# Finer parts of a weight split, earlier scatters and later transposes in a three-stage kernel

## The chip, the cores and the metric

The kernel runs on one core of one Trainium2 chip. The metric is the device time of one execution in microseconds; the time of a kernel is the median of several runs.

## The reference, cut to what matters

Three stages are chained over 4608 tokens of width 512. Attention without a softmax gives the rows `x`. A layer of eight experts adds to each row whose skip score is positive the gated output of its best expert. A dense layer follows, with the silu of one product between two. The inputs of the dense layer, `w_in` and `w_out`, are float64; the device reads them as pairs of 32-bit words.

```python
def _moe_ref(x, w_skip, w_gate, w1, w2):
    do_compute = (x @ w_skip) > 0
    xc = x[do_compute]
    ...
    for e in range(8):
        h = np.maximum(xc[mask] @ w1[e], 0.0)
        y[mask] = gate_w[mask, None] * (h @ w2[e])
    out[do_compute] = xc + y
def _moe2_ref(x, w_in, w_out):
    h = x @ w_in
    g = h * (1.0 / (1.0 + np.exp(-h)))
    return g @ w_out
```

## The kernel before, in words

The attention stage (to about 155 us) also sorts the tokens by expert. It stays as it is. What follows is one loop over **steps** (`steps`, the loop over `n` at the end). Steps 0 to 63 belong to eight **units** of eight steps, one unit per expert (`units`, kind "e"; unit 0 is steps 0 to 7). A unit has 384 down to 256 rows in three tiles (two in the last unit). From step 64 on come nine **groups** of 512 tokens and sixteen steps each (kind "g", the dense or GLU layer).

A step uses one **chunk** of weights: 128 of the hidden columns. In step n the tensor engine (PE) runs the first product of step n (`first`, L1194, twelve matmuls into `ph`), then the second product of step n - 1 (`second`, L1224, three matmuls per tile into `acc`). Each product is made of three, because both operands are split into a rounded part and a rest (`w[:, 0]`, `w[:, 1]`; `x` and `h` likewise). `h` leaves `ph` by ACT (L1200, the relu) and the vector engine DVE (L1201, the rest); in a GLU step by ACT, DVE, ACT, DVE in turn (L1206 to L1209). At the end of a unit DVE adds the result to the rows (`xe`, L1234); the rows are stored by a DMA on POOL's queue (L1239, units 0 to 5) or on SP's queue, and gathers on POOL's queue (L906, `fetch`) bring the rows of the unit after next into the buffers so freed.

**The weights.** SP's queue loads them into three staging buffers in the order of the list `order`, three tasks ahead (`load_ahead`). An expert's chunk is split by ACT (L143) and DVE (L144), two steps before its use. A chunk of the dense layer comes in two float64 **halves** (`w_in`, `w_out`). A half takes ACT's L153 and DVE's L154, L156, L158, L162, L166, then ACT's L177, two products on POOL (L178, L179) and one addition on DVE (L174). The `yield`s of `split` cut DVE's operations into parts. `split_on` issues L177 to L179 for halves whose parts are all issued, and L174 at its next call. Eleven chunks of the dense layer (22 halves) have buffers of their own and are split during the expert steps. The table `at_step` says when: whole halves in one go, at the third, fifth and seventh step of units 0 to 6, and one more at step 55. The other ten halves follow from step 64, by `split_slowly`, four parts of five a step.

**Turns.** The rows of the next unit are transposed on PE into `pt` (`turn`, L1149; two `pt` buffers), copied by ACT (L1158) and DVE (L1159) into `xT`. A unit's four turns come at its sixth step (one), seventh (two) and eighth (one), ahead of that step's first product; all four of unit 7 at its last step.

**Scatters.** `permute(t)` writes the place of 128 rows into the table `perm` by an indirect DMA on POOL's queue (L1138); six of them, at steps 2, 4, ... 12. Each writes the same tensor, so each waits until the one before has landed. The table is read back at step 24.

The schedule is manual: every engine executes its instructions in the order in which the program issues them. In a step that order is: turns, first product with its evictions, `split_on`, second product (in a unit's first step: the stores and gathers of the unit before), weight splits, then the scatter.

```python
        split_on()
        if n >= LAG:
            u2, f2, c2 = steps[n - LAG]
            second(u2, f2, c2, hs.pop(n - LAG))
            ...
        split_next(len(at_step.get(n, [])))
        if n >= NE:
            split_slowly(LAST_OPS)
```

Of the kernel before, what the change touches and what calls it, by code (L numbers as in the profile page):

```python
# [24 lines left out]
def tile_kernel(ctx, tc, q, k, v, g_norm, w_skip, w_gate, w1, w2, w_in, w_out, out):  # L25
# [3 lines left out]
    E = w_gate.shape[1]  # L29
# [13 lines left out]
    KD = DM // P  # L43
# [9 lines left out]
    KE = FE // P  # L53
# [3 lines left out]
    NWA = 3  # L57
# [27 lines left out]
    NP = GT + -(-CAPS[E - 1] // P)  # L85
# [51 lines left out]
    def split(task):  # L137


        t = staged.pop(task)  # L140
        w = part(task)
        if task[1] is None:
            nc.scalar.activation(w[:, 0, :], t.bitcast(F32), AF.Copy)  # L143
            nc.vector.tensor_tensor(w[:, 1, :], t.bitcast(F32), w[:, 0, :].bitcast(F32), ALU.subtract)  # L144
            yield
            return
        tv = t.rearrange("p (n o) -> p n o", o=2)
        hi, lo = tv[:, :, 1], tv[:, :, 0]
        vec = nc.vector
        x1 = xp.tile([P, DM], F32, tag="x", name="x1")  # L150
        x3 = xp.tile([P, DM], F32, tag="x", name="x3")
        x2 = xp.tile([P, DM], F32, tag="x", name="x2")
        nc.scalar.activation(x3, lo.bitcast(U32), AF.Copy, scale=2.0 ** -52)  # L153
        vec.tensor_scalar(x2.bitcast(I32), hi, 0x7FFFFFFF, None, ALU.bitwise_and)  # L154
        yield
        vec.scalar_tensor_tensor(x1, x2, SMALLEST, hi.bitcast(F32), ALU.is_ge, ALU.mult)  # L156
        yield
        vec.tensor_scalar(  # L158
            x2.bitcast(I32), x1.bitcast(I32), 3, 0x3FFFFFFF, ALU.logical_shift_left, ALU.bitwise_and
        )  # L160
        yield
        vec.scalar_tensor_tensor(  # L162
            x1.bitcast(I32), x1.bitcast(I32), -0x40000000, x2.bitcast(I32), ALU.bitwise_and, ALU.bitwise_or
        )
        yield
        vec.tensor_scalar(x2.bitcast(I32), x1.bitcast(I32), -0x800000, None, ALU.bitwise_and)  # L166
        begun.append((w, x1, x2, x3))
        yield
# [12 lines left out]

    NE = E * KE
    NCW = 2 * (NW - NWE)
    at_step = {}
    for n in range(NE - NWA):
        at_step.setdefault(n + 1, []).append((n + NWA, None))
    for i in range(NCW):
        n = (i // 3) * KE + 2 + 2 * (i % 3) if i < NCW - 1 else NE - KE - 1  # L190
        at_step.setdefault(n, []).append((NE + i // 2, i % 2))

    LAST_OPS = 4
    order = [(c, None) for c in range(NWA)] + [x for n in sorted(at_step) for x in at_step[n]]
    order += [(NE + i // 2, i % 2) for i in range(NCW, 2 * KF)]
    nload = [0]
    nsplit = [0]
# [15 lines left out]
    def split_slowly(n):  # L213
        while n:
            if not slow:
                if nsplit[0] == len(order):
                    return
                slow.append(split(order[nsplit[0]]))
                nsplit[0] += 1
            if next(slow[0], slow) is slow:  # L220
                slow.clear()
                split_on()
                load_ahead()
            else:
                n -= 1

# [922 lines left out]
    def turn(u, kk, pt=None):  # L1151
        if pt is None:
            pt = ps_t.tile([P, GN], F32, tag="t", name="pt")
            for s in range(len(tokens_of[u])):
                turn_tile(u, kk, s, pt)
        x = xtp.tile([P, 2, GN], F32R, tag="xT", name="xT")
        n = sum(tokens_of[u])
        nc.scalar.activation(x[:, 0, 0:n], pt[:, 0:n], AF.Copy)  # L1158
        nc.vector.tensor_tensor(x[:, 1, 0:n], pt[:, 0:n], x[:, 0, 0:n].bitcast(F32), ALU.subtract)  # L1159
        xT_of[u, kk] = x  # L1160
# [25 lines left out]
    def first(u, f, c):  # L1186
        kind, _ = units[u]
        n = sum(tokens_of[u])
        w = chunks[c]
        ph = ps_h.tile([P, GN], F32, tag="h", name="ph")  # L1190
        for kk in range(KD):
            x = xT_of[u, kk]
            for a, (wi, xi) in enumerate(((0, 0), (0, 1), (1, 0))):
                nc.tensor.matmul(  # L1194
                    ph[:, 0:n], w[:, wi, kk * P:(kk + 1) * P], x[:, xi, 0:n],
                    start=(kk == 0 and a == 0), stop=(kk == KD - 1 and a == 2),
                )
        h = hp_.tile([P, 2, GN], F32R, tag="h", name="h")
        if kind == "e":
            nc.scalar.activation(h[:, 0, 0:n], ph[:, 0:n], AF.Relu)  # L1200
            nc.vector.scalar_tensor_tensor(  # L1201
                h[:, 1, 0:n], ph[:, 0:n], 0.0, h[:, 0, 0:n].bitcast(F32), ALU.max, ALU.subtract
            )
        else:
            sg = sgp.tile([P, GN], F32, tag="sg", name="sg")
            nc.scalar.activation(sg, ph, AF.Sigmoid)  # L1206
            nc.vector.tensor_tensor(sg, ph, sg, ALU.mult)  # L1207
            nc.scalar.activation(h[:, 0, :], sg, AF.Copy)  # L1208
            nc.vector.tensor_tensor(h[:, 1, :], sg, h[:, 0, :].bitcast(F32), ALU.subtract)  # L1209
        return h  # L1210
# [53 lines left out]
    c = 0  # L1264
# [22 lines left out]
    for n in range(len(steps) + LAG):  # L1287
        now = steps[n] if n < len(steps) else None
        if now is not None:
            u, f, c = now  # L1290
            kind, i = units[u]
            nxt = u + 1
            if nxt < len(units):
                at = {"e": (5, 6, 6, 7), "g": (11, 12, 13, 14)}[kind] if u != E - 1 else (7, 7, 7, 7)
                for kk in range(KD):
                    if at[kk] == f and u < E:
                        turn(nxt, kk)
            hs[n] = first(u, f, c)
        split_on()
        if n >= LAG:  # L1300
            u2, f2, c2 = steps[n - LAG]
            second(u2, f2, c2, hs.pop(n - LAG))
            last = f2 == nf[units[u2][0]] - 1
            if last and u2 + 2 <= E:
                fetch(u2 + 2)
        split_next(len(at_step.get(n, [])))
        if n >= NE:
            split_slowly(LAST_OPS)
        if now is not None and E <= u < len(units) - 1:
            for s in range(GT):  # L1310
                if at[s] == f:
                    turn_blocks(nxt, s)
        if now is not None and nxt == E and f == at[0] - 1:
            sort_rows(nxt)
        if n == 0:
            row_of_place()
        elif n % 2 == 0 and n // 2 <= NP:
            permute(n // 2 - 1)
        if n == 31:
            prepare_blocks()  # L1320
        if n == 32:
            order_blocks()
        if n == 24:
            nc.sync.dma_start(inew, perm.rearrange("(p t) c -> p t c", p=P))
        if now is not None and kind == "g" and nxt < len(units) and f < 2 * GT:
            fetch_blocks(nxt, f)
# [30 lines left out]
```

## Time and profile before

| | us |
|---|---|
| runs: median (lowest to highest of 3) | 1242.16 (1241.41 to 1244.04) |
| profiled execution: time | 1243.42 |
| profiled execution: span | 1241.6 |
| PE busy | 1179.1 (95%) |
| DVE busy | 626.6 (50%) |
| ACT busy | 441.3 (36%) |
| POOL busy | 361.8 (29%) |

All durations below are of the one profiled execution; its time is the span and 1.8 us around it. Busy shares are means over stages with different limits; the expert steps run from 165 to 440 us, the GLU groups from 440 us to the end. The granted clock is given as a share of 2.4 GHz (1.00), the lower level is 1.2 GHz.

### The profile page before, as it was taken

Reading aid. Unit: us, or ns where it says so; the run is one execution under the profiler, and the core shown is the slowest. Engines: PE = TensorE matmul, PEld = TensorE weight load, DVE = VectorE, ACT = ScalarE, POOL = GpSimd, SP = SyncE. Lnnn points to the kernel's source line nnn. Section 1 sums busy time; section 2 is a strip of 40 time slices with the busy share of each in tenths; the row PEclk is TensorE's granted clock in tenths of the full one; section 3 lists DMA queues with packets and bytes.
Section 4 is the critical chain, followed back from the end, with each engine's and each line's share of the span. In section 5 each row is a group of like instructions: output and inputs, shape, how many; then the busy total and the mean of one; then the engine's idle time right before and its main releaser. Section 6 shows DMA issues by size and latency. Waiting matters only on the chain.

```text
span 1241.6 us, 17430 instructions
## 1 busy us (share of the span) xinstructions
PE 1179.1 (95%) x6506; PEld 981.1 (79%) x6506; DVE 626.6 (50%) x1234; ACT 441.3 (36%) x902; POOL 361.8 (29%) x348
## 2 busy tenths in 40 slices
PE   8888399799999899999999999999999999999998
PEld 7777388688877787788888888888888888888886
DVE  3578967678878768732422423423423324324322
ACT  3666344344445433322322322322323223223222
POOL 1666434444454337333050220310400500400000
PEclk9999689899999899999999999999999999999999
DMA  9998457577777733010020010100200200200001
GB/s 238 282 282 307 170 169 207 148 214 213 209 213 217 218 92 92 1 45 24 1 64 5 16 54 1 54 15 1 64 6 1 68 1 1 68 1 1 35 1 34
DMA packets 108662, 118.83 MB, mean 96 GB/s; under 512 B 21872, under 2 KB 87408, under 8 KB 107552
## 3 DMA queue, kind: packets, MB, share of 16 engines
q1 hardware_dynamic: 99152, 97.17, 27.0%
q0 software_dynamic: 8064, 20.48, 5.8%
q8 instruction: 52, 0.85, 0.3%
q14 instruction: 34, 0.28, 0.1%
q10 hardware_dynamic: 1360, 0.05, 0.1%
HBM read 93.46 MB, written 24.21 MB: 95 GB/s over the span
## 4 chain that ended last, share of the span: by engine, by line
PE 70%; DVE 8%; issue 3%; DMA 2%; ACT 2%; POOL 1%; SPq 0%; DVEq 0%; ACTq 0%; POOLq 0%
PE ph L1194 35%; PE acc L1224 35%; DVE x L156 1%; DVE w L144 1%; DVE x L162 1%; PE pt L1149 1%; DVE h L1209 1%; DMA stg<-in_moe_w_in_dram 1%; DVE sg L1207 1%; POOL x L179 1%; DVE w L174 1%; ACT h L1208 1%; DVE x L154 1%; DVE x L158 1%; DMA stg_None<-in_moe_w_dram 0%
## 5 line engine op out<-in xcount | busy, mean ns | idle before, releaser
L1224 PE MATMUL acc<-w,h 128*128 128x512 f32 x2280 | 561.0, 393 | 6.4 <-DVE h L1209 1.9
L1194 PE MATMUL ph<-xT,w 128*128 128x512 f32 (+7 forms) x2496 | 546.4, 368 | 0.4 <-DVE w L144 0.4
L1194 PEld LDWEIGHTS ph<-xT,w 128*128 128x128 f32 x2496 | 443.3, 189 | 77.5 <-DVE w L144 0.7
L1224 PEld LDWEIGHTS acc<-w,h 128*128 128x128 f32 x2280 | 419.6, 185 | 103.4 <-DVE h L1209 3.2
L1207 DVE TENSOR_TENSOR sg<-ph,sg 128x512 f32<-128x512 f32 x144 | 99.5, 691 | 377.2 <-ACT sg L1206 377.2
L940 POOL DMA_INDIRECT x<-xs,qidx x128 | 127.5, 996 | 386.0 <-DVE turned L1179 308.9
L1206 ACT ACTIVATE sg<-ph 128x512 f32<-128x512 f32 x144 | 86.0, 597 | 388.6 <-PE ph L1194 385.2
L1209 DVE TENSOR_TENSOR h<-sg,h 128x512 fp32r<-128x512 f32 x144 | 102.8, 714 | 100.7 <-ACT h L1208 94.4
L1208 ACT ACTIVATE h<-sg 128x512 fp32r<-128x512 f32 x144 | 91.1, 633 | 123.3 <-DVE sg L1207 123.3
L144 DVE TENSOR_TENSOR w<-stg_None,w 128x1024 fp32r<-128x1024 f32 x64 | 80.9, 1266 | 19.4 <-ACT w L143 19.1
L178 POOL TENSOR_TENSOR x<-x,x 128x512 f32<-128x512 f32 x32 | 41.6, 1299 | 122.8 <-DVE x L166 109.7
L143 ACT ACTIVATE w<-stg_None 128x1024 fp32r<-128x1024 f32 x64 | 67.1, 1050 | 14.7 <-issue 9.0
L1200 ACT ACTIVATE h<-ph 128x304 fp32r<-128x304 f32 (+6 forms) x64 | 27.9, 436 | 100.4 <-PE ph L1194 98.7
L179 POOL TENSOR_TENSOR x<-x,w 128x512 f32<-128x512 f32 x32 | 62.3, 1945 | 0.5 <-ACT w L177 0.5
L574 POOL TENSOR_TENSOR rows<-rows,inv 128x512 f32<-128x512 f32 x33 | 35.0, 1062 | 64.6 <-DVE inv L557 34.9
L1201 DVE SCALAR_TENSOR_TENSOR h<-ph,h 128x304 fp32r<-128x304 f32 (+6 forms) x64 | 31.0, 484 | 29.9 <-ACT h L1200 29.9
L1183 ACT ACTIVATE xT<-turned 128x128 fp32r<-128x128 f32 x128 | 29.1, 298 | 46.6 <-DVE turned L1179 46.6
L402 PE MATMUL po<-wt,qT 128*128 128x146 f32 x256 | 40.9, 303 | 1.6 <-ACT wt L383 1.1
L576 POOL TENSOR_TENSOR rows<-rows,grow 128x512 f32<-128x512 f32 x33 | 40.6, 1230 | 2.6
L402 PEld LDWEIGHTS po<-wt,qT 128*128 128x128 f32 x256 | 36.3, 202 | 3.5 <-ACT wt L383 1.9
L1184 DVE TENSOR_TENSOR xT<-turned,xT 128x128 fp32r<-128x128 f32 x128 | 30.2, 298 | 12.1 <-ACT xT L1183 12.1
L177 ACT ACTIVATE w<-x 128x512 fp32r<-128x512 f32 x32 | 20.2, 630 | 34.2 <-DVE x L162 33.9
(186 smaller groups left out, 736.8 us busy)
## 6 DMA issues: line engine op xcount, KB each, us to landing
stg_None<-in_moe_w_dram SPq DMA_DIRECT2D x128, 256.0 KB, 3.3
xs<-rows SPq DMA_DIRECT2D x8, 1032.0 KB, 7.8
stg<-in_moe_w_in_dram SPq DMA_DIRECT2D x64, 128.0 KB, 3.9
stg<-in_moe_w_out_dram SPq DMA_DIRECT2D x16, 512.0 KB, 4.6
k<-in_k_dram SPq DMA_DIRECT2D x7, 1024.0 KB, 9.9
v<-in_v_dram SPq DMA_DIRECT2D x7, 1024.0 KB, 11.4
q<-in_q_dram SPq DMA_DIRECT2D x7, 1024.0 KB, 12.0
out_dram<-o SPq DMA_DIRECT2D x26, 256.0 KB, 2.4
```

What stands on the lines that cost most here:

```text
L143: nc.scalar.activation(w[:, 0, :], t.bitcast(F32), AF.Copy)
L144: nc.vector.tensor_tensor(w[:, 1, :], t.bitcast(F32), w[:, 0, :].bitcast(F32), ALU.subtract)
L178: nc.gpsimd.tensor_tensor(x3, x3, x2, ALU.mult)
L179: nc.gpsimd.tensor_tensor(x1, x1, w[:, 0, :].bitcast(F32), ALU.subtract)
L402: nc.tensor.matmul(po[i // 2][:, (i % 2) * 2 * DC:(i % 2 + 1) * 2 * DC], qT[:, i, :], w[:, 4 * hh + i, :], start=True, stop=True,)
L940: nc.gpsimd.indirect_dma_start(out=rows_of[u][s][:, a * XQ:(a + 1) * XQ], out_offset=None, in_=xblocks, in_offset=bass.IndirectOffsetOnAxi ...
L1194: nc.tensor.matmul(ph[:, 0:n], w[:, wi, kk * P:(kk + 1) * P], x[:, xi, 0:n], start=(kk == 0 and a == 0), stop=(kk == KD - 1 and a == 2),)
L1206: nc.scalar.activation(sg, ph, AF.Sigmoid)
L1207: nc.vector.tensor_tensor(sg, ph, sg, ALU.mult)
L1208: nc.scalar.activation(h[:, 0, :], sg, AF.Copy)
L1209: nc.vector.tensor_tensor(h[:, 1, :], sg, h[:, 0, :].bitcast(F32), ALU.subtract)
L1224: nc.tensor.matmul(accs[u, s][0:m], h[:, hi, s * P:s * P + m], w[:, wi, DM:2 * DM], start=(f == 0 and a == 0), stop=(last and a == 2),)
```

## The change

A half's parts become four (the first two DVE operations go together). The table `at_step` goes. From step 1 on, every expert step runs a fixed number of parts through `split_slowly`: two up to step 15, then one and two in turn; three in GLU steps. The list `order` is made from the same count, so that a half is listed where its first part falls due. An expert's chunk is split by `split_next(1)`, as before two steps ahead. The call of `split_on` that follows a half's last part can now come at the end of `split_slowly` in an expert step too. The six scatters move to steps 1 to 6. The turns of units 0 to 6 move behind the first product of their step; those of unit 7 stay.

```diff
@@ split
         vec.tensor_scalar(x2.bitcast(I32), hi, 0x7FFFFFFF, None, ALU.bitwise_and)
-        yield
         vec.scalar_tensor_tensor(x1, x2, SMALLEST, hi.bitcast(F32), ALU.is_ge, ALU.mult)
...
-    at_step = {}
-    for n in range(NE - NWA):
-        at_step.setdefault(n + 1, []).append((n + NWA, None))
-    for i in range(NCW):
-        n = (i // 3) * KE + 2 + 2 * (i % 3) if i < NCW - 1 else NE - KE - 1
-        at_step.setdefault(n, []).append((NE + i // 2, i % 2))
-
-    LAST_OPS = 4
-    order = [(c, None) for c in range(NWA)] + [x for n in sorted(at_step) for x in at_step[n]]
+    PARTS = 4
+
+    def parts_of_step(n):
+        return (2 if n < 2 * KE else 1 + n % 2) if n < NE else 3
+
+    order = [(c, None) for c in range(NWA)]
+    nparts = 0
+    for n in range(1, NE):
+        if n + NWA - 1 < NE:
+            order.append((n + NWA - 1, None))
+        for _ in range(parts_of_step(n)):
+            i, begins = divmod(nparts, PARTS)
+            if i < NCW and not begins:
+                order.append((NE + i // 2, i % 2))
+            nparts += 1
...
@@ split_slowly
-                if nsplit[0] == len(order):
+                if nsplit[0] == len(order) or order[nsplit[0]][1] is None:
+                    return
+                c = order[nsplit[0]][0]
+                if c - NE >= NCW // 2 and now_at[0] < NE:
                     return
...
@@ the loop over steps
-                for kk in range(KD):
-                    if at[kk] == f and u < E:
-                        turn(nxt, kk)
+            turned = [kk for kk in range(KD) if nxt < len(units) and u < E and at[kk] == f]
+            if u == E - 1:
+                for kk in turned:
+                    turn(nxt, kk)
             hs[n] = first(u, f, c)
+            if u < E - 1:
+                for kk in turned:
+                    turn(nxt, kk)
...
-        split_next(len(at_step.get(n, [])))
-        if n >= NE:
-            split_slowly(LAST_OPS)
+        now_at[0] = n
+        if 1 <= n <= NE - NWA:
+            split_next(1)
+        split_slowly(parts_of_step(n))
...
-        elif n % 2 == 0 and n // 2 <= NP:
-            permute(n // 2 - 1)
+        elif n <= NP:
+            permute(n - 1)
```

## Rows read from the trace of the kernel before

**Rows 1.** Windows: units 1, 2, 7, GLU groups 0, 1; busy us, clock, DMA.

```profile
core 0: us, PE busy (x) PEld busy (x) DVE busy (x) ACT busy (x) POOL busy (x), PEclk, DMA share, GB/s
198.77:240.97 42.20, 35.81 (x181) 31.71 (x180) 26.90 (x42) 16.67 (x27) 18.33 (x16) 0.92 0.63 170
240.97:274.89 33.92, 33.92 (x181) 28.71 (x180) 26.73 (x41) 16.76 (x27) 15.43 (x13) 1.00 0.76 216
...
406.90:440.30 33.40, 29.06 (x165) 24.67 (x163) 23.60 (x34) 14.53 (x24) 11.09 (x8) 0.90 0.65 196
440.30:527.34 87.04, 83.69 (x356) 67.17 (x354) 68.17 (x105) 31.01 (x61) 44.73 (x36) 0.98 0.22 61
527.34:614.99 87.65, 87.65 (x386) 72.10 (x385) 30.66 (x57) 24.98 (x52) 20.23 (x20) 1.00 0.08 25
```

**Rows 2.** Waits of PE, whole span: us in total, times, longest us.

```profile
PE pt L1149 <- DVE xT L1159: 9.7, 6, 6.4
```

**Rows 3.** Timeline of POOL in unit 1: start us, us, what [idle before <-releaser].

```profile
212.68 1.01 POOL L1138 DMA_INDIRECT perm<-mine,goes  x1 [0.30 <-issue]
221.46 1.00 POOL L1138 DMA_INDIRECT perm<-mine,goes  x1 [7.76 <-DMA perm<-mine,goes]
...
223.73 1.25 POOL L179 TENSOR_TENSOR x<-x,w 128x512 f32<-128x512 f32 x1
```

**Rows 4.** Timeline of DVE in unit 1.

```profile
225.02 0.69 DVE L174 TENSOR_TENSOR w<-x,x 128x512 fp32r<-128x512 f32 x1 [6.99 <-POOL x L179]
```

**Rows 5.** Timeline of PE in unit 1 (steps 9, 11, 13 and 14).

```profile
202.81 2.10 PE L1194 MATMUL ph<-xT,w 128*128 128x352 f32 x12
...
210.80 2.09 PE L1194 MATMUL ph<-xT,w 128*128 128x352 f32 x12
...
219.09 2.17 PE L1194 MATMUL ph<-xT,w 128*128 128x352 f32 x12
...
230.03 0.82 PE L1149 MATMUL pt<-ident,xe 128*128 128x128 f32 x3 [6.39 <-DVE xT L1159]
230.58 3.87 PE L1194 MATMUL ph<-xT,w 128*128 128x352 f32 x12
```

**Rows 6.** Groups of DVE by line, units 2 to 6: busy us, mean ns.

```profile
L144 DVE TENSOR_TENSOR w<-stg_None,w 128x1024 fp32r<-128x1024 f32 x40 | 51.1, 1278 | 12.6 <-ACT w L143 12.5
L1201 DVE SCALAR_TENSOR_TENSOR h<-ph,h 128x304 fp32r<-128x304 f32 (+3 forms) x39 | 18.5, 475 | 13.9 <-ACT h L1200 13.9
...
L156 DVE SCALAR_TENSOR_TENSOR x<-x,stg 128x512 f32<-128x512 f32 x15 | 10.4, 692 | 0.5
L174 DVE TENSOR_TENSOR w<-x,x 128x512 fp32r<-128x512 f32 x15 | 10.3, 687 | 2.6 <-POOL x L179 2.3
...
L158 DVE TENSOR_SCALAR x<-x 128x512 int32<-128x512 int32 x15 | 6.4, 427 | 0.5
```

**Rows 7.** Groups of POOL by line, units 2 to 6.

```profile
L179 POOL TENSOR_TENSOR x<-x,w 128x512 f32<-128x512 f32 x15 | 33.1, 2210 | 0.0
L178 POOL TENSOR_TENSOR x<-x,x 128x512 f32<-128x512 f32 x15 | 19.3, 1289 | 71.8 <-DVE x L166 67.1 <-PE pt L1149 4.7
```

**Rows 8.** Timeline of unit 2: POOL's last gather, PE's first product of step 20.

```profile
252.08 0.91 POOL L906 DMA_INDIRECT xe<-xs,gidx  x1 [0.30 <-issue]
256.73 2.00 PE L1194 MATMUL ph<-xT,w 128*128 128x336 f32 x12
```

**Rows 9.** Waits of PE from 235 to 430 us: us in total, times, longest.

```profile
PE pt L1149 <- DVE xT L1159: 2.3, 4, 0.9
```

**Rows 10.** Timeline of PE in unit 7 (steps 57, 59 and 60).

```profile
410.42 1.59 PE L1194 MATMUL ph<-xT,w 128*128 128x256 f32 x12
...
423.00 1.59 PE L1194 MATMUL ph<-xT,w 128*128 128x256 f32 x12
...
425.81 1.57 PE L1194 MATMUL ph<-xT,w 128*128 128x256 f32 x12
```

**Rows 11.** Timeline of DVE and PE in the first GLU group.

```profile
473.32 3.53 DVE L1209 TENSOR_TENSOR h<-sg,h 128x512 fp32r<-128x512 f32 x1 [0.70 <-ACT h L1208]
...
476.90 4.15 PE L1224 MATMUL acc<-w,h 128*128 128x512 f32 x10 [1.94 <-DVE h L1209]
```

## The prediction before the result was known

> **What bounds the kernel now.** I read the page first, then TensorE's (PE's) waits, then windows cut at the units of the step loop, then the timelines of PE, POOL and DVE around each loss. The reader is to see that PE is the bound, and where it isn't fed. From the second GLU group on nothing can be won: all 87.65 us of a group are PE work at full clock [rows 1], and the change touches only what comes earlier. Unit 1 (steps 8 to 15) takes 42.20 us with 35.81 busy at clock 0.92, while unit 2, with steps almost as long, takes 33.92 and is full. Unit 7 holds 29.06 busy of 33.40 at clock 0.90; the first GLU group 83.69 of 87.04 at 0.98 [rows 1]. PE's longest single wait in these stages, 6.4 us, is a transpose waiting for the vector engine's (DVE's) xT, and six such waits make 9.7 us [rows 2]. So what DVE delivers late is what PE lacks.
>
> The loss of unit 1 is a chain through POOL. The fourth scatter starts at 212.68, behind the gathers; the fifth waits 7.76 us for it to land and stands ahead of a half's two products on POOL's queue [rows 3]. DVE's addition of that half waits 6.99 us for them [rows 4], the evictions behind it too, and PE stands 6.39 us. The next twelve products then take 3.87 us [rows 5] against 2.17 in the same unit at full clock, 1.70 more, so 8.1 in all.
>
> **The change, part by part.** My sum goes by units, against the profiled execution (1243.42 us, of which 1241.6 are span), which lies 1.26 above the median shown (1242.16); the difference is then taken off the median.
>
> *Scatters at steps 1 to 6.* Six scatters move ahead of the first unit's stores and gathers; POOL is otherwise nearly empty there. They still queue with three halves' products (L178, L179) and wait for each other's landing, so a half can be held for about a scatter's 1.0 us [rows 3]. I price unit 0 at +0.3, bounds 0 and +2. The 8.1 us of unit 1 lose their cause.
>
> *The stream, unit 1.* Following the new list of parts: halves begin at steps 1, 3, 5, ... 15 and then every 2 2/3 steps. A half whose fourth part ends a step has its POOL products issued behind the next step's first product, and its DVE addition in that same step, where before a whole step lay between. That is a new wait. In unit 1 it meets the gathers: half 3 ends at step 8, its products are issued at step 9, behind the stores and gathers that step 8 put on POOL. These end at 212.38 in the old trace (the scatter at 212.68 shows 0.30 idle before it) [rows 3], 9.6 us after step 9 began at 202.81 [rows 5]. Then L178 1.29 [rows 7], L179 1.25 (as beside a waiting DVE [rows 3]), addition 0.69, and ahead of the next eviction the new half's two parts, 0.43 + 0.69 + 0.43 (the first taken like the third), and the eviction itself, 0.48 [rows 6]: h of step 10 is there at about 217.6. PE wants it when step 11's first product ends, 210.80 + 2.0 = 212.8 [rows 5]. So some 4.8 us of new stall, and 1.7 for the slow clock after it, as after the old one [rows 5]: 6.5 where 8.1 went. Unit 1 gains 1.6. Bounds: +2 (DVE also has four halves instead of three here) and -8.1 (no wait).
>
> *Unit 2.* DVE leaves unit 1 behind. A half costs it three operations of 0.43 and three of 0.69, 3.36, a step's eviction and chunk 0.48 + 1.28 [rows 6]: two steps with one half 6.9 of PE's 8.1 us, before turns, xe and the waits for POOL. Nothing catches up before the stream slows at step 16. I put +3.0 on unit 2; bounds 0 and +5.
>
> *Units 2 to 6, steady.* Three halves fill exactly eight steps, so the pattern repeats: one half's products are issued at the end of each unit's second step, behind the gathers, and added in the third. In unit 2 the gathers end at 252.99; plus 1.29 + 1.25, the addition 0.69 and the chunk behind it 1.28, chunk 20 is whole at 257.5. PE begins with it at 256.73 and needs its second plane at the third product, 257.05 [rows 8]: 0.45 of stall. Later units have shorter steps; I take 0.6 a unit, 3.0 over five. Against it stand four waits at the third turn of a unit, in units 3 to 6, 2.3 us together, the longest 0.9 [rows 9]. They come from DVE's burst of five operations ahead of the first turn's xT, which the stream spreads. Net +0.7; bounds -2.3 and +10 (below).
>
> *The turns.* Behind the first product, the same transposes and copies run; the eviction of h comes ahead of them on ACT and DVE, and xT comes about 2 us later. Price 0: the second product and three quarters of the next unit's first one come before the last xT is used and cover it. If DVE is so late that this cover is gone, the last turn makes PE wait for what is missing, by estimate 0.5 a unit, which lies inside the bounds above.
>
> *Unit 7.* Before, halves 20 and 21 run in the last two steps of unit 6, whole bursts, and DVE arrives in unit 7 with additions, xe and chunks queued. From 410.42 to 423.00 PE makes two steps, which take 2.81 each when fed [rows 10]: 12.58 - 5.62 = 7.0 lost. Now half 21's last part is at step 54 and its addition at 55, and no part runs from 56 to 63. I take -7.0; bounds -3 and -7.
>
> *First GLU group.* Three of four parts a step instead of four of five: 0.75 half a step for 0.8. The same ten halves end one step later, in the steps in which the next group's blocks are turned. PE loses 3.35 idle [rows 1] and, after 1.94 of it, some 1.9 at the low clock (ten products in 4.15) [rows 11]. I take -1.0; bounds -4 and +3. Here a row and a rule can be weighed: DVE's subtraction took 3.53 us [rows 11] against 0.69 for an addition of the same size [rows 6], while POOL ran a half's two products, and POOL's L179 takes 2.21 on average [rows 7] but 1.25 while DVE waits [rows 3]. So the two engines pay for each other, and I don't count the thinner stream as relief in full.
> The Trainium skill (SBUF — State Buffer, section Who interferes with whom) says that a DVE instruction with two SBUF inputs and a GpSimd instruction that reads SBUF exclude each other through a shared port: the later one blocks fully. By that rule the ten halves cost the two engines the same whatever the spread, and this term would be 0, the sum 1.0 higher; these rows agree with it, though no row here isolates the port.
>
> Smaller edits: the joined first two operations free the staging buffer no later; the loads keep their order of splits. Nothing is added. Price 0, bounds -1 and +1.
>
> **Sum.** +0.3 - 1.6 + 3.0 + 0.7 - 7.0 - 1.0 = -5.6: 1243.42 to 1237.8 in a profiled execution, 1236.6 as a median.
>
> **Rivals.**
> *The gathers set the pace (slower).* If the gathers on POOL end some 2 us later after xe than in unit 2, because DVE evicts xe late, each of units 2 to 6 pays 0.45 + 2 = about 2.5 at its fifth step, 12.5 in all instead of 3.0, and unit 1 gains nothing: -5.6 + 9.5 + 1.6 = +5.5, 1247.7. It decides from the point at which the five stalls exceed about 9 us together. For it: POOL is in order and every unit has one half behind its gathers; DVE has little slack. Against it: in unit 2 the gathers end within half a us of harmless. Chance 0.22.
> *The block behind the gathers isn't felt (much faster).* If DVE's queue reaches the addition only when POOL is through, unit 1 gains 8.1, unit 2 loses nothing and units 2 to 6 gain 2.3: +0.3 - 8.1 - 2.3 - 7.0 - 1.0 = -18.1, 1224.1. For it: the old stall's cause is plainly gone. Against it: 4.8 us in unit 1 follow from program order alone. Chance 0.12.
> *Exclusion sets the pace (no change).* If DVE and POOL can't overlap, units 0 and 1, which get 7.5 halves in 16 steps instead of 6, pay 1.5 x (1.29 + 1.25) = 3.8 more: 1236.6 + 3.8 = 1240.4. The skill's rule named above would bring that about. For it: the 3.53 us. Against it: units 2 to 6 run full with three halves already. Chance 0.13.
> *The stream stalls.* It returns when the next task on the list is a chunk; then halves slip into the GLU group, and what unit 7 gains is lost there: -5.6 + 7.0 = +1.4, 1243.6. Counting parts against the list, every half is listed where its first part falls due, so 0.03.
>
> **How the numbers follow.** The forecast has 0.50. Below 1225 lies most of the much faster case, above 1247 half of the slower one, together not 2 in 10. The forecast's own range, by the bounds of units 1, 2 and the GLU group, is 1229 to 1243. A measurement of this kernel can tell 0.2%, 2.5 us. Faster: 0.45 of the forecast, 0.12, and 0.05 of the exclusion case: 0.62. Slower: 0.22, and 0.03 from the upper ends of the forecast and of exclusion: 0.25. The same: the rest, 0.13, with the stalled stream in it.
>
> **What would show it.** Right: no scatter waits behind gathers; unit 7 near 26.5 us with PE full; in unit 1 POOL's L178 right behind the last gather, DVE's L174 waiting for L179 for over 5 us, PE standing about 5 us ahead of an accumulation; in each of units 2 to 6 a wait under 1 us for a chunk's DVE plane at the fifth step. Wrong: unit 1 full, or units 2 to 6 over 2 us longer each, or unit 7 as long as before.

## The result, and the profile after

The changed kernel takes 1254.46 us (median of five runs, 1251.84 to 1260.11) against 1242.16 of the kernel before (five runs, 1241.41 to 1244.77). The ratio is 1.0103, with an interval of 1.0074 to 1.0131: slower by one per cent, where a gain of 5.6 us was forecast. The profiled execution is the longest of the five, 1260.11 us with a span of 1258.3, so its span is 16.7 us above that of before, where the medians are 12.3 apart.

Windows cut at the units answer [rows 1]: first units 1 to 5, then unit 7 and the first GLU group, in the columns of [rows 1].

```profile
core 0: us, PE busy (x) PEld busy (x) DVE busy (x) ACT busy (x) POOL busy (x), PEclk, DMA share, GB/s
203.12:243.59 40.47, 35.09 (x182) 30.50 (x181) 29.83 (x47) 16.79 (x29) 16.29 (x14) 0.96 0.61 183
243.59:282.84 39.25, 36.29 (x182) 30.12 (x180) 27.23 (x44) 17.42 (x28) 16.11 (x14) 0.96 0.68 195
282.84:319.60 36.76, 34.99 (x182) 29.15 (x180) 26.84 (x42) 16.21 (x27) 12.58 (x13) 0.95 0.63 194
319.60:357.42 37.82, 35.44 (x190) 29.06 (x188) 27.22 (x46) 15.91 (x27) 12.31 (x13) 0.95 0.62 188
357.42:393.89 36.47, 34.27 (x181) 27.89 (x180) 25.68 (x42) 16.30 (x27) 13.25 (x13) 0.95 0.62 193
426.96:456.87 29.91, 27.22 (x164) 23.97 (x163) 18.47 (x25) 12.45 (x21) 5.90 (x5) 0.94 0.68 190
456.87:543.99 87.12, 84.13 (x355) 65.36 (x354) 64.66 (x102) 30.82 (x61) 44.11 (x36) 1.00 0.22 61
```

The next table sets these lengths beside those of before and beside the kernels of the experiments. Each length runs from the start of one unit's first product to that of the next, in the PE timeline of one profiled execution.

| us | unit 0 | 1 | 2 | 3 | 4 | 5 | 6 | 2 to 6 | 7 | GLU group 0 |
|---|---|---|---|---|---|---|---|---|---|---|
| before | 33.67 | 42.20 | 33.92 | 33.60 | 33.88 | 33.18 | 31.35 | 165.9 | 33.40 | 87.04 |
| after | 34.21 | 40.47 | 39.25 | 36.76 | 37.82 | 36.47 | 33.07 | 183.4 | 29.91 | 87.12 |
| e1, scatters alone | 34.38 | 33.40 | 33.94 | 33.33 | 33.44 | 35.38 | 30.96 | 167.1 | 34.58 | 87.07 |
| e2, gathers later | 34.15 | 35.63 | 36.21 | 35.52 | 33.76 | 34.16 | 30.51 | 170.2 | 27.57 | 87.04 |
| e3, additions later | 33.90 | 40.14 | 35.07 | 33.36 | 34.17 | 32.80 | 34.12 | 169.5 | 27.57 | 86.92 |
| e4, stream paused | 33.60 | 38.31 | 35.04 | 33.85 | 34.59 | 33.33 | 32.72 | 169.5 | 28.33 | 87.69 |
| e5, stream shifted | 33.88 | 37.42 | 33.92 | 33.17 | 33.40 | 32.48 | 30.58 | 163.6 | 27.15 | 88.17 |
| e11, changed again | 33.21 | 41.29 | 37.16 | 36.74 | 36.24 | 34.74 | 35.16 | 180.0 | 26.46 | 88.49 |

Between the two kernels, 3.8 of the 16.7 us lie ahead of step 0, where nothing was edited; unit 0 adds 0.5, unit 1 gives 1.7, units 2 to 6 cost 17.4, unit 7 gives 3.5, and the GLU group 0.1. The loss is in units 2 to 6. PE's idle time there grew from 165.93 - 163.59 = 2.3 us to 11.9 (183.37 less 171.52 busy), and its busy time by 7.9 us for the same matmuls, at a granted clock of 0.95 and 0.96 in units 2 to 5, where before had 1.00 in all five. In unit 6 the clock stayed at 1.00.

The waits of PE over the whole span answer [rows 2] (us in total, times, longest):

```profile
PE ph L1206 <- DVE w L144: 11.7, 6, 2.5
PE acc L1236 <- DVE h L1213: 5.4, 1, 5.4
...
PE pt L1161 <- DVE xT L1171: 1.0, 1, 1.0
```

The transposes' wait of 9.7 us is down to 1.0, and the four short waits of [rows 9] are gone. In their place stand six waits of the first product for a chunk's plane, which DVE's L144 writes. One of them, of 0.47 us, lies at unit 2's third step. The timeline of PE shows the five others, one at the fifth step of each of units 2 to 6; its first row is the wait of unit 1, for `h` (brackets: idle before, and its releaser).

```profile
223.09 3.32 PE L1236 MATMUL acc<-w,h 128*128 128x512 f32 x7 [5.38 <-DVE h L1213]
...
263.32 2.79 PE L1206 MATMUL ph<-xT,w 128*128 128x336 f32 x10 [2.48 <-DVE w L144]
265.92 2.86 PE L1236 MATMUL acc<-w,h 128*128 128x512 f32 x9
...
300.47 2.33 PE L1206 MATMUL ph<-xT,w 128*128 128x320 f32 x10 [1.77 <-DVE w L144]
...
338.62 2.69 PE L1206 MATMUL ph<-xT,w 128*128 128x304 f32 x10 [2.26 <-DVE w L144]
...
375.14 1.82 PE L1206 MATMUL ph<-xT,w 128*128 128x304 f32 x10 [2.20 <-DVE w L144]
376.76 3.66 PE L1236 MATMUL acc<-w,h 128*128 128x512 f32 x9
...
411.53 1.60 PE L1206 MATMUL ph<-xT,w 128*128 128x288 f32 x10 [2.54 <-DVE w L144]
```

The five add up to 11.25 us. After the first four the matmuls run long: the nine of the next second product, 2.26 us behind the stall of unit 6, took 2.86, 3.24, 2.81 and 3.66 in units 2 to 5. That is the second part of the bill, the 7.9 us at the lower clock. So the 17.4 are about 11.7 of waits and 7.9 of slow matmuls, less the 2.3 of [rows 9] that are gone.

The chain behind the wait of unit 4, in the timeline of POOL:

```profile
324.87 1.88 POOL L1251 DMA_DIRECT2D xs<-xe  x3 [5.04 <-DVE xe L1246]
330.64 1.02 POOL L918 DMA_INDIRECT xe<-xs,gidx  x1 [3.90 <-DMA xs<-xe]
331.97 0.98 POOL L918 DMA_INDIRECT xe<-xs,gidx  x1 [0.30 <-issue]
333.25 0.88 POOL L918 DMA_INDIRECT xe<-xs,gidx  x1 [0.30 <-issue]
334.15 1.31 POOL L177 TENSOR_TENSOR x<-x,x 128x512 f32<-128x512 f32 x1
335.42 1.28 POOL L178 TENSOR_TENSOR x<-x,w 128x512 f32<-128x512 f32 x1
```

and of DVE:

```profile
336.73 0.69 DVE L173 TENSOR_TENSOR w<-x,x 128x512 fp32r<-128x512 f32 x1 [5.47 <-POOL x L178]
337.34 1.22 DVE L144 TENSOR_TENSOR w<-stg_None,w 128x1024 fp32r<-128x1024 f32 x1
```

POOL issues the stores, cannot issue the gathers before these have landed, and issues the half's two products (L177, L178) right behind the last gather. DVE's addition (L173) waits 5.47 us for them and holds the chunk (L144) that PE needs: PE goes on at 338.62, when L144 ends. (L177, L178 and L173 of this kernel are L178, L179 and L174 of the kernel before.) It is the chain of the forecast, link for link. What differs is the time at which the gathers end. The same place in unit 4 of the kernel before:

```profile
313.68 1.88 POOL L1239 DMA_DIRECT2D xs<-xe  x3 [2.38 <-DVE xe L1234]
317.45 1.09 POOL L906 DMA_INDIRECT xe<-xs,gidx  x1 [1.89 <-DMA xs<-xe]
```

POOL stands idle ahead of a unit's first gather, until the rows stored by the unit before have landed: 1.78, 1.92, 1.89, 1.04 and 2.81 us in units 2 to 6 before, 9.4 together, and 2.23, 2.71, 3.90, 3.14 and 4.28 now, 16.3 together.

Measured from the unit's start, the last gather ended after 12.0, 11.8, 12.5, 11.6 and 11.4 us in units 2 to 6 before, and after 15.3, 13.1, 14.5, 13.2 and 13.2 now. In unit 2 the stores themselves come 2.2 us later (DVE behind, as forecast). In units 3 to 6 they come 0.1 to 0.3 us later; nearly all the rest is the wait for their landing.

The trace also shows what else moved there. SP's queue issues the load of a `w_in` half in unit 4, first before, then now:

```profile
315.85 2.00 SPq L123 DMA_DIRECT2D stg<-in_moe_w_in_dram  x4
```

```profile
322.65 1.77 SPq L123 DMA_DIRECT2D stg<-in_moe_w_in_dram  x4
```

In units 2 to 6 the load of the next half was issued 2.1 to 2.3 us behind the first store; now it goes out 1.7 to 2.3 us ahead of it. From the first store to the first gather of unit 4 the DMA engines were busy to a share of 0.60 before and of 0.93 now (last two numbers: share and GB/s):

```profile
313.68:317.45 3.77, 3.77 (x23) 3.16 (x22) 3.76 (x6) 1.37 (x2) 1.76 (x4) 1.00 0.60 180
```

```profile
324.87:330.64 5.77, 5.77 (x36) 5.08 (x35) 5.74 (x10) 2.77 (x5) 1.75 (x3) 1.00 0.93 259
```

Over the five units the share is 0.54 to 0.69 before and 0.81 to 0.98 now.

### The profile page after: what moved, and what is told of

It is laid out like the page before. It is cut to its first block, busy times and chain, and to the rows that moved or that the text cites. A ratio compares the mean times of both kernels' runs of the same rounds, so it can differ in the third digit from the quotient of the medians.

```text
span 1258.3 us, 17437 instructions
## 1 busy us (share of the span) xinstructions
PE 1188.8 (94%) x6506; PEld 986.3 (78%) x6506; DVE 621.7 (49%) x1234; ACT 439.7 (35%) x902; POOL 349.6 (28%) x348
## 4 chain that ended last, share of the span: by engine, by line
PE 69%; DVE 7%; POOL 5%; issue 4%; DMA 2%; ACT 1%; SPq 0%; DVEq 0%; ACTq 0%; POOLq 0%
PE ph L1206 34%; PE acc L1236 34%; POOL x L178 2%; DVE w L144 1%; POOL x L177 1%; DVE x L155 1%; POOL xe L918 1%; PE pt L1161 1%; DMA xg<-xs,inew 1%; DVE w L173 1%; DVE sg L1219 1%; DVE xe L1246 1%; DVE x L161 1%; DVE x L154 1%; DMA stg<-in_moe_w_in_dram 0%
## 5 line engine op out<-in xcount | busy, mean ns | idle before, releaser
L1206 PE MATMUL ph<-xT,w 128*128 128x512 f32 (+7 forms) x2496 | 546.9, 368 | 11.7 <-DVE w L144 11.7
L1221 DVE TENSOR_TENSOR h<-sg,h 128x512 fp32r<-128x512 f32 x144 | 99.9, 694 | 100.6 <-ACT h L1220 95.0
L144 DVE TENSOR_TENSOR w<-stg_None,w 128x1024 fp32r<-128x1024 f32 x64 | 84.3, 1318 | 19.7 <-ACT w L143 19.5
L143 ACT ACTIVATE w<-stg_None 128x1024 fp32r<-128x1024 f32 x64 | 67.3, 1054 | 23.5 <-DMA stg_None<-in_moe_w_dram 14.5
L177 POOL TENSOR_TENSOR x<-x,x 128x512 f32<-128x512 f32 x32 | 41.7, 1304 | 116.6 <-DVE x L165 100.9
L178 POOL TENSOR_TENSOR x<-x,w 128x512 f32<-128x512 f32 x32 | 48.7, 1521 | 7.0 <-ACT w L176 7.0
L173 DVE TENSOR_TENSOR w<-x,x 128x512 fp32r<-128x512 f32 x32 | 21.9, 686 | 42.6 <-POOL x L178 42.6
L1196 DVE TENSOR_TENSOR xT<-turned,xT 128x128 fp32r<-128x128 f32 x128 | 30.5, 300 | 12.1 <-ACT xT L1195 12.1
```

The source lines that it names most:

```text
L177: nc.gpsimd.tensor_tensor(x3, x3, x2, ALU.mult)
L178: nc.gpsimd.tensor_tensor(x1, x1, w[:, 0, :].bitcast(F32), ALU.subtract)
L1206: nc.tensor.matmul(ph[:, 0:n], w[:, wi, kk * P:(kk + 1) * P], x[:, xi, 0:n], start=(kk == 0 and a == 0), stop=(kk == KD - 1 and a == 2),)
```

## The experiments

On the chips of the experiments the kernel before took 1250.6 to 1252.5 us, so ratios are compared, each to the kernel before on the same chip. **The theory** after the result: program order. A half's products stand behind the gathers on POOL, its addition ahead of the next chunk on DVE, and the gathers end too late. **The rival**: exclusion or load, that DVE and POOL have more work that cannot overlap, wherever it stands.

### e1: the scatters alone

```diff
 (kernel before)
-        elif n % 2 == 0 and n // 2 <= NP:
-            permute(n // 2 - 1)
+        elif n <= NP:
+            permute(n - 1)
```

> The kernel before with the six scatters at steps 1 to 6 and nothing else. Theory (the scatters cost unit 1 its 8.1 us and nothing replaces them there): unit 1 falls from 42.2 to about 34 us, the other units stay within 0.5; about 1234 us. Rival (POOL's queue is full around the gathers anyway and another wait takes the place): unit 1 gains less than 3, about 1240 or more.

Measured: 0.9946 (0.9917 to 0.9974), 1243.55 against 1250.57 us. Unit 1 falls from 42.20 to 33.40 us. The 8.1 us put on the old scatters in unit 1 were theirs (8.8 measured), and this part of the change is worth a half per cent by itself. Not all other units stayed within 0.5: units 0, 5 and 7 took 0.7, 2.2 and 1.2 us more. So the rest of the change costs some 1.6% on top.

### e2: the gathers behind the products

The gathers of the rows of units 2 to 7 are issued at the end of the second step of the unit before, behind that step's parts, instead of in its first.

```diff
 (changed kernel)
-            if last and u2 + 2 <= E:
-                fetch(u2 + 2)
+            if last and u2 + 2 == E:
+                fetch(E)
...
         split_slowly(parts_of_step(n))
+        if n % KE == 1 and KE < n < NE - KE:
+            fetch(n // KE + 1)
```

> The changed kernel with the gathers of units 1 to 6 issued behind the second step's parts instead of the first step's second product, so that no half's POOL products queue behind gathers. Theory (the halves behind the gathers are the loss): the waits of PE for a chunk at the fifth step (11.7 us in six) and for h in unit 1 (5.4 us) go, with the slow clock after each; units 1 to 6 come to 33 or 34 us each at most; about 1228 us, less what later gathers cost in turns that wait for rows (bounds 0 and 10). Rival (DVE and POOL exclude each other, or DVE is simply full): the same work stands on both engines, units 2 to 6 stay within 1 us of the changed kernel, about 1252.

Measured: 0.9964 (0.9938 to 0.9990). Units 2 to 6 take 170.2 us where the changed kernel took 183.4, with every DVE and POOL instruction still there. Timeline of POOL in unit 2:

```profile
252.12 1.75 POOL L178 TENSOR_TENSOR x<-x,w 128x512 f32<-128x512 f32 x1
254.02 1.52 POOL L918 DMA_INDIRECT xe<-xs,gidx  x1 [0.15 <-PE ph L1206]
```

Waits of PE from 169 to 425 us:

```profile
PE pt L1161 <- DMA xe<-xs,gidx: 4.4, 4, 2.3
...
PE ph L1206 <- DVE w L144: 0.5, 1, 0.5
```

The wait for the chunk falls from 11.7 us to 0.5 (at unit 2's third step), and what is late next shows itself: the rows, gathered later, now hold the transposes 4.4 us. So units 1 to 3, at 35.5 to 36.2 us, miss the 33 or 34 expected.

### e3: the additions later

POOL keeps the order of the changed kernel; DVE makes a half's addition two or three steps after its products, so that its chunks no longer stand behind them.

```diff
 (changed kernel)
-    def split_on():
+    def split_on(behind=2):
...
-        while halfway:
-            w, x1, x3 = halfway.pop(0)
+        n = now_at[0]
+        while halfway and (n >= NE - 1 or n == 31 or n - halfway[0][3] >= halfway[0][4]):
+            w, x1, x3, _, _ = halfway.pop(0)
...
-            halfway.append((w, x1, x3))
+            halfway.append((w, x1, x3, n, behind))
...
-                split_on()
+                split_on(3 if now_at[0] >= 2 * KE else 2)
```

> The changed kernel with each half's DVE addition issued two or three steps after its POOL products instead of in the same or the next step (one half, at step 31, excepted); the gathers stay where they are. Theory (DVE waits in order for products that stand behind gathers): unit 1's stall of 5.4 us shrinks under 1.5, the waits at the fifth step under 0.5 each; about 1230 us. Rival (load or exclusion): no change within 3 us of the changed kernel, about 1254.

Measured: 0.9962 (0.9933 to 0.9990); units 2 to 6 169.5 us. The chain is cut at another link, and the gain is that of e2 within the intervals. But two waits at the fifth step are left, above the bounds expected: 2.07 us in unit 6 and 2.90 in unit 1, which stays at 40.14 us. Timelines of POOL, DVE and PE there:

```profile
216.27 1.28 POOL L178 TENSOR_TENSOR x<-x,x 128x512 f32<-128x512 f32 x1
217.50 1.25 POOL L179 TENSOR_TENSOR x<-x,w 128x512 f32<-128x512 f32 x1
```

```profile
216.40 3.45 DVE L144 TENSOR_TENSOR w<-stg_None,w 128x1024 fp32r<-128x1024 f32 x1 [2.64 <-ACT w L143]
```

```profile
219.91 3.30 PE L1207 MATMUL ph<-xT,w 128*128 128x352 f32 x10 [2.90 <-DVE w L144]
```

DVE no longer waits for the products in program order, and yet it loses that time: its L144, 1.22 us when POOL rests, took 3.45 while POOL ran the two in a row. In unit 6 an L144 took 3.41 in the same way. The Trainium skill (SBUF — State Buffer, section Who interferes with whom) has a DVE instruction with two SBUF inputs and a GpSimd instruction that reads SBUF shut each other out of a shared port; these rows agree, though they don't isolate the port. So the rival is real as a price, 2.2 us where such an operation falls on PE's path, but in units 2 to 6 of e3 only the L144 of unit 6 cost PE as much, and it isn't what set their pace.

### e4 and e5: the stream moved in time

Both have four halves in unit 0, three in each of units 1 to 6, and no part in unit 7. e4 stops the stream around the gathers and doubles it between. e5 keeps the rate in units 1 to 6 and shifts it: one and two parts in turn, begun anew at step 8, so that a unit's first products fall ahead of its stores and the next ones at its fourth step.

```diff
 (changed kernel, e4)
-        return (2 if n < 2 * KE else 1 + n % 2) if n < NE else 3
+        if n >= NE:
+            return 3
+        return (0, 2, 2, 2 + (n < KE), 2 + (n < KE), 2, 2, 2 * (n < KE))[n % KE] if n < NE - KE else 0
 (changed kernel, e5)
-        return (2 if n < 2 * KE else 1 + n % 2) if n < NE else 3
+        if n >= NE:
+            return 3
+        return (0, 2, 2, 3, 3, 2, 2, 2)[n] if n < KE else 1 + n % 2 if n < NE - KE else 0
```

> The changed kernel with another count of parts: unit 0 runs 0, 2, 2, 3, 3, 2, 2, 2 parts in its eight steps, units 1 to 6 run 0, 2, 2, 2, 2, 2, 2, 0, unit 7 none, so that halves end at the third, fifth and seventh step and no product falls behind gathers by more than the gathers' last us. Theory: as with later gathers, units 1 to 6 at 33 to 34 us, about 1228 us. Rival (load or exclusion): the total of DVE and POOL work is the same and denser in the middle steps, so it stays above 1245.

Measured: 0.9987 (0.9961 to 1.0012), no difference from the kernel before, and a miss. The waits for the chunk fell to 1.6 us in all, but seven waits of the transposes for xT make 4.6 us, and unit 1 takes 38.31: two parts in each of six steps may put DVE behind where the turns come, which no run isolates. Its units 2 to 6 are as long as those of e2 and e3.

> The changed kernel with another phase of the stream: unit 0 runs 0, 2, 2, 3, 3, 2, 2, 2 parts (four whole halves), every later unit to the seventh one and two in turn, unit 7 none. Halves then end at the third, sixth and eighth step of a unit; the same parts, the same rate from unit 2 on, the gathers where they are. Theory (one half in three stands behind the gathers): units 2 to 6, 183.4 us in the changed kernel, come to about 168; unit 1 to about 34.5; about 1.5% under the changed kernel, 0.5% under the kernel before on the same chip. Rival (a stream of fine parts is itself slower, by waits for POOL in the same step): units 2 to 6 stay above 176, and the time at or above the kernel before.

Measured: 0.9908 (0.9876 to 0.9940), 1240.68 against 1251.52 us: faster than both kernels, though unit 1, at 37.42, misses the 34.5 expected. Windows of units 1 to 3 and the timeline of POOL into unit 2:

```profile
198.82:236.24 37.42, 34.73 (x181) 29.35 (x180) 31.46 (x49) 16.83 (x26) 15.66 (x13) 1.00 0.71 212
236.24:270.16 33.92, 33.92 (x181) 28.80 (x180) 27.04 (x42) 16.54 (x26) 12.70 (x12) 1.00 0.77 218
270.16:303.33 33.17, 33.17 (x181) 27.85 (x180) 27.57 (x42) 16.42 (x26) 12.94 (x12) 1.00 0.73 222
```

```profile
239.52 1.30 POOL L178 TENSOR_TENSOR x<-x,w 128x512 f32<-128x512 f32 x1
240.76 1.70 POOL L1253 DMA_DIRECT2D xs<-xe  x3
244.12 1.03 POOL L920 DMA_INDIRECT xe<-xs,gidx  x1 [1.66 <-DMA xs<-xe]
...
247.23 0.91 POOL L920 DMA_INDIRECT xe<-xs,gidx  x1 [0.30 <-issue]
250.67 1.29 POOL L177 TENSOR_TENSOR x<-x,x 128x512 f32<-128x512 f32 x1 [2.53 <-ACT h L1214]
```

Units 2 and 3 are full: PE busy is the whole window, at full clock. POOL's first products now stand ahead of the stores, the next ones 2.5 us clear of the last gather. Units 2 to 6 take 163.6 us, 2.4 less than before, which is about the four short waits of [rows 9]. Three halves a unit cost PE nothing where they are rightly placed; the rival of exclusion or load falls for units 2 to 6. Here the halves' loads no longer go out just ahead of the stores; between the first store and the first gather the DMA share is 0.60 to 0.72, and POOL's wait for the landing is 1.66 to 2.74 us, about as in the kernel before.

### e6: whole bursts, with another place for two of them

The kernel before with the early scatters and four halves in unit 0, at steps 1, 3, 5 and 7; after it three a unit as before, so that the last one comes at step 54 and none at step 55.

```diff
 (kernel before, with the diff of e1)
-        n = (i // 3) * KE + 2 + 2 * (i % 3) if i < NCW - 1 else NE - KE - 1
+        n = 1 + 2 * i if i < 4 else (i - 1) // 3 * KE + 2 + 2 * ((i - 1) % 3)
```

> The kernel before with the scatters at steps 1 to 6 and whole halves as before, but four in unit 0 (steps 1, 3, 5, 7), three in each of units 1 to 6 and none at step 55. Theory (unit 7 lost 7 us to the halves squeezed in ahead of it): unit 7 falls from 33.4 to 27 us, the rest as with the scatters alone; another 0.5% under that kernel, 1.0% under the kernel before. Rival (unit 7 waits for the last unit's rows to land, whatever DVE does): unit 7 stays above 30.

Measured: 0.9958 (0.9934 to 0.9982). Unit 7 takes 27.60 us instead of 33.40, with whole bursts elsewhere: what cost it 6 us was the burst at step 55, right behind that of step 54, and the stream isn't needed to win them back. Unit 1 gave 2.8 us back (36.24 against e1's 33.40). Units 0 to 7 are still 5.6 us shorter than in e1's profile, yet by the ratios the whole stands no better than e1: another half per cent was expected and isn't there. Its profile begins step 0 at 169.74 us, e1's at 164.35, a stage that no edit touches; whether that hides the gain in the medians too isn't shown.

### e7 and e8: the changed kernel with one part undone

e7 has the scatters at steps 2, 4, ... 12 again; e8 has the turns ahead of the first product again. One execution of each was taken.

```diff
 (changed kernel, e7)
-        elif n <= NP:
-            permute(n - 1)
+        elif n % 2 == 0 and n // 2 <= NP:
+            permute(n // 2 - 1)
 (changed kernel, e8)
-            if u == E - 1:
-                for kk in turned:
-                    turn(nxt, kk)
+            for kk in turned:
+                turn(nxt, kk)
             hs[n] = first(u, f, c)
-            if u < E - 1:
-                for kk in turned:
-                    turn(nxt, kk)
```

> The changed kernel with the scatters back at steps 2, 4, ... 12. Theory (scatters behind gathers hold POOL): unit 1's stall grows from 5.4 us by the scatter's wait, 4 to 8 us more, unit 1 at 45 to 50; the other units as in the changed kernel. Rival (the half behind the gathers is blocked so long that the scatters hide in it): unit 1 within 2 us of 40.5.

Measured: 1271.58 us; unit 1 takes 42.12, as the rival has it. PE's wait there is 7.09 us where the changed kernel had 5.38 and 5.67 in two profiles. With the stream in place the early scatters are worth one or two us of unit 1, not the 8.8 of e1: the half behind the gathers stands in the same place as the scatter did, and PE's loss has changed owner.

> The changed kernel with the turns ahead of the first product again. Theory (the turns cost nothing and save nothing by themselves): units 2 to 6 within 1 us each of the changed kernel, with waits of a third turn for xT of 0.3 to 1 us in some. Rival (the late turns are what delays evictions and chunks): units 2 to 6 fall by 2 us or more each.

Measured: 1257.93 us. Waits of PE in units 0 to 7:

```profile
PE ph L1206 <- DVE w L144: 12.1, 5, 3.0
PE acc L1236 <- DVE h L1213: 6.2, 1, 6.2
```

The five waits are there as in the changed kernel (12.1 against 11.7 us), so the moved turns have no part in them. Units 2 to 6 take 182.9 us together against 183.4; single units differ by up to 2.0, more than the 1 expected: unit 2 ran at a clock of 1.00 here and of 0.96 there.

### e9 and e10: variants of e5

e9 is e5 with the turns ahead of the first product, by the diff of e8. e10 is e5 with unit 0 front-loaded:

```diff
 (e5)
-        return (0, 2, 2, 3, 3, 2, 2, 2)[n] if n < KE else 1 + n % 2 if n < NE - KE else 0
+        return (0, 3, 3, 3, 3, 2, 2, 0)[n] if n < KE else 1 + n % 2 if n < NE - KE else 0
```

> The shifted stream with the turns ahead of the first product again. Theory (late turns save waits at the third turn of a unit and cost a wait for the last xT where DVE is late): unit 1 loses its first wait (1.6 us), units 3 to 6 get back third-turn waits of 0 to 0.6 each; within 0.2% of the shifted stream. Rival (the turns carry part of the gain): units 2 to 6 longer by 3 us or more together, 0.3% or more slower than the shifted stream.

Measured: 0.9934 (0.9913 to 0.9955), which overlaps with e5's interval: whether the turns' new place gains anything isn't told apart. Units 2 to 6 take 164.4 us against 163.6.

> The shifted stream with unit 0 running 0, 3, 3, 3, 3, 2, 2, 0 parts, so that its fourth half ends a step before unit 1 begins. Theory (unit 1's 37.4 us are a backlog of DVE from the unit's end): unit 1 falls by 1 to 3 us, unit 0 rises by 0 to 1. Rival (the backlog is the load of four halves, wherever they stand): the two units together stay within 0.7 us of 71.3.

Measured: 0.9915 (0.9887 to 0.9944), the same as e5 within the intervals. Unit 1 falls from 37.42 to 33.61 us, and unit 0 rises from 33.88 to 36.70: the two together are 70.31 against 71.30. That is neither the 1 to 3 and 0 to 1 us of the theory nor within 0.7, as the rival had it, but nearer to the rival: most of what unit 1 wins, unit 0 loses.

### e11: the changed kernel again

No edit; taken since the profile of the changed kernel was the longest of its runs.

> The changed kernel once more, on the chip of the two others. Theory: its stalls follow from program order, so units 2 to 6 again hold a wait of about 2 us for a chunk at the fifth step, and the time is 1.0% above the kernel before, within 0.4; the shifted stream kernels lie 1.5% or more below it. Rival (the first measurement caught an odd state): within 0.3% of the kernel before.

Measured: 1.0104 (1.0059 to 1.0150), as in the first comparison. On this chip e9 and e10 took 1245.47 and 1241.48 us, 1.8 and 2.1% less than its 1267.81. Timeline of PE, units 2 to 6:

```profile
264.77 1.80 PE L1206 MATMUL ph<-xT,w 128*128 128x336 f32 x10 [2.49 <-DVE w L144]
...
300.36 2.88 PE L1206 MATMUL ph<-xT,w 128*128 128x320 f32 x10 [1.77 <-DVE w L144]
...
408.64 1.85 PE L1206 MATMUL ph<-xT,w 128*128 128x288 f32 x10 [3.09 <-DVE w L144]
```

With 2.22 and 2.03 us in units 4 and 5 the five are 11.6 us together, in an execution of its own: they come from the program, not from one execution. The slow matmuls are less steady: here the clock fell after two of the five stalls only (0.95 in units 3 and 6), and units 2 to 6 are busy 168.1 us, 4.5 above the kernel before instead of 7.9.

## Why the prediction was wrong

**Units 2 to 6: the step that failed.** The working took the end of the gathers from the trace of before and made of it 0.6 us of stall a unit: net +0.7, with +3.0 for unit 2's backlog. They cost 17.4. The chain itself was right, and the stalls follow from it once the gathers' real end is put in. In units 3 to 6 the gathers ended 1.3, 2.0, 1.6 and 1.7 us later than before; 0.45 more than each gives 1.8, 2.5, 2.1 and 2.2, where 1.77, 2.26, 2.20 and 2.54 were measured. In unit 2 they ended 3.2 us later and PE came 1.0 later, which gives 2.7 where 2.48 was measured. So the input was at fault: a time that hangs on another queue was read from a kernel in which that queue had other traffic, and a margin of half a us was trusted to hold. That the wait for the landing of the stores rose is shown (9.4 to 16.3 us). Beside it stands a term put at nothing: "the loads keep their order of splits", price 0. The order held, the time did not: the next half's load now goes out just ahead of the stores instead of just behind them, and the DMA share there, 0.54 to 0.69 before, is 0.81 to 0.98. In e5, where that load lies elsewhere, share and wait are near those of before. These rows fit a load that delays the landing; since e5 moves the products too, no run isolates it, and this cause stays argued.

Of the +3.0 for unit 2's backlog, 0.47 us shows as a wait of its own; beyond that it shows only in the stores, 2.2 us later. The forecast's range had no room for the miss: it was built from the bounds of unit 1, unit 2 and the GLU group, and left out this term's own upper bound of +10, which the 14.4 us besides the 3.0 exceed as well.

The second miss in the same term is the clock. In unit 1 the working added 1.7 us for the slow matmuls after a stall. For the stalls of units 2 to 6 it added nothing, nor did the rival's price. The windows show 7.9 us more of busy time in the first profile and 4.5 in e11's.

**The rival that won.** "The gathers set the pace" decided at five stalls of more than 9 us together, at the fifth step, about 2.5 each: they are 11.25, at that step. Its 1247.7 is 6.8 below the median. In units 2 to 6 it had 3.0 + 12.5 - 2.3 = 13.2 us, 4.2 short of the 17.4, with no slow clock in it and a backlog that hardly shows; that unit 1 gains nothing is wrong, and unit 7 gave half. So the place and the size of the stalls are right, and the total is near in part by luck. Its reason, xe evicted late, holds in unit 2 alone.

**Unit 1** (-1.6 forecast, -1.7 measured) is right, in cause too: the half behind the gathers, DVE waiting 5.93 us for L178, PE standing 5.38 us where 4.8 was put:

```profile
220.39 0.69 DVE L173 TENSOR_TENSOR w<-x,x 128x512 fp32r<-128x512 f32 x1 [5.93 <-POOL x L178]
```

The gathers ended later here too, 14.7 us into the unit where 13.6 was taken over, but no margin hung on it. The forecast treated this stall as certain and those of units 2 to 6 as nearly nothing, though both are the same chain with a different margin.

**Unit 7** (-7.0, to 26.4): 26.46 in the second profile of the changed kernel, 27.15 in e5. In the first profile it is 29.91. There POOL and PE show:

```profile
436.67 1.73 POOL L938 DMA_INDIRECT xg<-xs,inew  x1 [8.73 <-DMA xs<-xe]
```

```profile
449.79 0.77 PE L1161 MATMUL pt<-ident,sorted 128*128 128x128 f32 x5 [1.40 <-DVE sorted L1181]
```

The rows of the first GLU group could be gathered only when the last stores had landed, and its transposes waited. DVE's copy of these rows waited 1.97 us for their gather. Seven us is thus what the term brings where these rows come in time; in this profile half of it was lost again.

**Scatters.** The 8.1 us are confirmed by e1, where nothing else was changed. In the changed kernel they bring little, as the sum had it (6.5 of new stall where 8.1 went). **Unit 0**: +0.3 forecast, +0.5 measured. **The turns**, at 0, fit: the third-turn waits are gone, and without the moved turns e8 takes the same time in units 2 to 6 together. **GLU group 0**: -1.0 forecast, +0.1 measured; but this group takes 86.5 to 88.5 us over the profiles of the changed kernel and the experiments, so one pair of profiles can't tell -1.0 from 0.

**Ahead of step 0** the profiles differ by 3.8 us of the 16.7, with no edit there. Over the twelve profiled executions of the changed kernel and the experiments the first step begins between 163.8 and 171.1 us, and the changed kernel alone has 168.9 and 171.1. What sets this stays open.

## What to carry to other kernels

When work is put on an in-order engine behind something that waits for another queue, ask what that wait will be in the changed kernel and how much margin is left: half a microsecond, read from the old trace, is none. Ask also when a reordered load will run, not only in which order. Price each new stall with the slow matmuls that may follow it; here they added seven tenths to the five stalls in one profile and four tenths in another. And before thinning out work to relieve an engine, try its phase: at the same rate, begun at another step, the parts cost units 2 to 6 nothing (163.6 us instead of 183.4). With that, and with the count of parts changed in units 0 and 1, a loss of 1.0% became a gain of 0.9%.

## What was not expected of the hardware

DVE can stand still while POOL runs two products in a row, also where nothing in the program orders the two: 3.45 us for L144 in e3, 3.53 in e5, against 1.22 for the same operation when POOL rests. Timelines of DVE and POOL in unit 0 of e5:

```profile
195.80 3.53 DVE L144 TENSOR_TENSOR w<-stg_None,w 128x1024 fp32r<-128x1024 f32 x1
```

```profile
195.70 1.29 POOL L177 TENSOR_TENSOR x<-x,x 128x512 f32<-128x512 f32 x1
196.95 1.30 POOL L178 TENSOR_TENSOR x<-x,w 128x512 f32<-128x512 f32 x1
```

Here the loss isn't shared: POOL's two take 1.29 and 1.30, as beside a waiting DVE, and DVE takes all of the 2.3 us. In other places it is POOL that pays: at the start of unit 2 of the changed kernel its L178 took 2.28 us beside an L144 of 1.33. The forecast had the two pay for each other without asking which; where the operation held is the one that makes PE's next chunk, that matters more than the sum. Over the thirteen profiles 122 L144 lie beside both products of a half, and the rows show an order. In 104 of them L144 began 0.06 to 0.32 us ahead of the first product's end: it took 1.22 to 1.41 us, and the second product 2.25 to 2.36. Eleven took 2.80 to 3.80, with the second product at its usual 1.25 to 1.32; all of these began 0.46 us or more ahead of that end. Three others that began so early paid on both sides (1.71 to 1.97, and 2.27 to 2.29), so what decides it was not isolated.
